# Retention feeding two feed-forward layers: where the decays are applied, and how the first product is placed between the retention steps

## The chip, the cores and the metric

The kernel runs on one core of one Trainium2 chip. The metric is the device time of one execution in microseconds (us), median of three runs.

## The reference, cut to what matters

Inputs q, k, v are 4 x 8 x 768 x 64 (batch, heads, sequence, head size). For every batch and head a state of 64 x 64 decays and grows along the sequence, and the outputs go through two dense layers:

```python
gamma = 1.0 - 2.0 ** (-5.0 - np.arange(H))
for t in range(S):
    state = gamma * state + outer(k[t], v[t])
    y[t] = scale * (q[t] @ state)
x = y.transpose(0, 2, 1, 3).reshape(3072, 512)
x = leaky_relu(x @ w_in) @ w_out          # 512 -> 2048 -> 512
x = sigmoid_gated(x @ w2_in) @ w2_out     # 512 -> 2048 -> 512
```

## The kernel before, in words

The first stage computes the retention in 24 steps (4 batches of 6 chunks of 128 positions) and, beside it, the first product (x @ w_in) of the first block of 512 tokens. Everything behind it is dense matrix work on TensorE (PE): the rest of the first product (line 238), then the three other products (lines 776 and 583). The change touches the first stage alone. In program order each engine runs its own queue, so the order in which the Python code issues work is the order on each engine.

One retention step s does the following. `a_scores` (line 269) multiplies keys and queries of 8 heads on PE (line 277) into PSUM banks 0 and 1, and VectorE (DVE) multiplies the result by the causal mask into SBUF (line 280). `a_decay` (line 283) multiplies the keys by their decays on ScalarE (ACT), eight instructions a step (line 288), two steps ahead. `a_out` (line 290) runs on PE the state update (kv, line 300, not in the last chunk of a batch), the output inside the chunk (line 307), and the output from the state (line 313, not in a batch's first chunk). DVE forms the next state from kv (line 316); kv accumulates over the chunks in one bank, so the next kv waits for line 316. The output lies in two PSUM banks; two such pairs take turns (banks 3 to 6). `a_store` (line 320) multiplies the output by the decays of the queries (`qdec`) on DVE: line 332, three instructions, for blocks 0 and 1, line 345, one, for later blocks, which go to DRAM. For block 0 ACT makes the rounded high part (line 341) and GpSimd (POOL) subtracts for the low part (line 151). Half of the rows come out with the two 64-row halves exchanged; `swapped` (line 159) puts them right, by three DMAs for each store and for `qdec`.

A weight tile of the first product goes through: `load_raw` (line 165, one DMA of 512 KB), `convert` (two instructions on ACT, lines 172 and 173, four on DVE, lines 176 to 182), `round_up` (line 191, on POOL for the first two tiles, on DVE for the others), `finish` (ACT copy, line 154, DVE subtraction, line 151). One tile is then 12 matmuls of 128 x 512 (`ffn_in`, line 231), a Lrelu on ACT out of bank 7 (line 242) and a store. From step 6 on, 16 of the 18 steps end with one tile. Loads of q, k, v (1 MB a step, line 267, on SP's DMA queue) are four steps ahead.

Of the kernel before, what the change touches and what calls it, by code (L numbers as in the profile page):

```python
# [21 lines left out]
P = 128  # L22
# [65 lines left out]
def retention_two_ffn(ctx: ExitStack, tc: tile.TileContext, qkv, consts, small, w1i, w1o, w2i, w2o, scratch, out):  # L88
# [123 lines left out]
    W0 = 6  # L212
    now_in = [[m for m in range(KF) if W0 + m * (N_STEPS - W0) // KF == s] for s in range(N_STEPS)]
    done = [0]

    def work_first(n):
        if n + 2 < KF:
            load_raw(n + 2)
        if n < KF:
            convert(n)  # L220

    def work_last(n):
        if n < KF:
            round_up(*conv[n], nc.gpsimd if n < 2 else nc.vector)
        if 0 < n <= KF:
            finish(n - 1)

    h_banks = [7]
    i_h = [0]

    def ffn_in(blk, m, place=None):
# [9 lines left out]
        t = next(g_ring) if place is None else place  # L241
        nc.scalar.activation(out=t, in_=h, func=AF.Lrelu)  # L242
        if place is None:
            nc.scalar.dma_start(out=gd1[m][:, blk * TB : blk * TB + TB], in_=t)

    def retention():
# [12 lines left out]
        ins, sc_t, ks_t = {}, {}, {}  # L259
        kv = banks[:, 2, : NP * D].rearrange("p (n d) -> p n d", n=NP)  # L260
        o_ring = itertools.cycle([banks[:, 3:5], banks[:, 5:7]])
# [21 lines left out]
        def a_decay(s):  # L283
            b, c = steps[s]
            if c < NC - 1:
                ks_t[s] = ins[s][:, 2].rearrange("p (h d) -> p h d", h=H)
                for h in range(H):
                    nc.scalar.activation(out=ks_t[s][:, h], in_=ks_t[s][:, h], func=AF.Copy, scale=kdec[:, c, h : h + 1])

        def a_out(s):  # L290
            b, c = steps[s]
            t = ins.pop(s)
            sm, ks = sc_t.pop(s), ks_t.pop(s, None)
# [8 lines left out]
            o = next(o_ring)  # L302
# [15 lines left out]
            return o  # L318

        def a_store(s, o):  # L320
# [4 lines left out]
            else:  # L325
# [4 lines left out]
            def put(r, u, t):  # L330
                n = 2 * P
                nc.vector.tensor_tensor(out=x[r].rearrange("p (m u) i -> p u m i", u=2)[:, u],  # L332
                                        in0=o[t, u, :n].rearrange("p (m i) -> p m i", i=P),
# [9 lines left out]
            if blk < 2:  # L343
                return
# [773 lines left out]
```

## Time and profile before

| what | value |
|---|---|
| median of 3 runs | 1048.61 us (1048.59 to 1049.26) |
| profiled execution: span from first to last instruction | 1047.2 us |
| PE busy | 1038.1 us (99%) |
| DVE busy | 821.6 us (78%) |
| ACT busy | 578.2 us (55%) |
| POOL busy | 72.8 us (7%) |

The page gives the profiled execution's own time as its span, 1047.2 us; the median lies 1.4 us above it, which is what lies around the span. A view that shows starts gives them in us from the start of the span. "PE ... x16" in a timeline is sixteen matmul records: a 4-byte product of the retention leaves two records for each matmul. A matmul's modelled end overlaps the next start, so durations on PE are taken from start to start.

### The profile page before, as it was taken

What the parts mean: (1) busy time and instruction counts of PE and PEld (TensorE: products, weight loads), DVE (VectorE), ACT (ScalarE), POOL (GpSimd) and SP (SyncE); (2) the same over time, 40 slices, a digit from 0 to 9 for tenths busy, and PEclk for the clock granted to TensorE, in tenths of its full rate; (3) what the DMA queues carried; (4) which work ended last, traced back from release to release, by engine and by line L of the source; (5) the groups of instructions that cost most, each with busy time, mean ns of one, the idle gap of its engine ahead of it and who ended that gap; (6) DMA issues with size and microseconds to landing.
All of it is one profiled execution on the core that took longest, in us unless ns stands there. A gap on an engine that the chain in (4) does not pass through costs nothing.

```text
span 1047.2 us, 16899 instructions
## 1 busy us (share of the span) xinstructions
PE 1038.1 (99%) x5955; PEld 892.3 (85%) x5955; DVE 821.6 (78%) x1425; ACT 578.2 (55%) x1111; POOL 72.8 (7%) x75
## 2 busy tenths in 40 slices
PE   8999999999999999999999999999999999999998
PEld 6778788888888888888888999999999888888886
DVE  5998749886885798787789677686768898887986
ACT  5766446554554654544546566565657564545443
POOL 2100000000000000000000104434410000000000
PEclk9999999999999999999999999999999999999999
DMA  9989577999996423524429846647487735635624
GB/s 336 364 318 363 212 232 236 317 320 323 326 334 207 151 81 131 191 80 161 160 81 331 302 160 212 230 171 282 158 271 263 250 101 139 184 92 143 168 81 80
DMA packets 168645, 223.72 MB, mean 214 GB/s; under 512 B 57328, under 2 KB 113392, under 8 KB 165360
## 3 DMA queue, kind: packets, MB, share of 16 engines
q1 hardware_dynamic: 133696, 175.67, 51.3%
q10 hardware_dynamic: 34864, 46.97, 12.2%
q8 instruction: 46, 0.75, 0.3%
q14 instruction: 39, 0.32, 0.1%
HBM read 137.66 MB, written 84.93 MB: 213 GB/s over the span
## 4 chain that ended last, share of the span: by engine, by line
PE 94%; DVE 3%; DMA 2%; issue 0%; ACT 0%; ACTq 0%; SPq 0%
PE psum L776 41%; PE psum L238 25%; PE psum L583 22%; PE psum L277 2%; PE psum L307 2%; DMA h<-qkv 1%; PE psum L300 1%; PE psum L313 1%; ACTq L1000 0%; DVE c L992 0%; DVE c L784 0%; DVE e L151 0%; DVE a L151 0%; DVE d L151 0%; DVE c L332 0%
## 5 line engine op out<-in xcount | busy, mean ns | idle before, releaser
L776 PE MATMUL psum<-c,h 128*128 128x512 f32 x1008 | 228.8, 389 | 0.0
L776 PEld LDWEIGHTS psum<-c,h 128*128 128x128 f32 x1008 | 189.2, 188 | 39.3
L776 PE MATMUL psum<-e,h 128*128 128x512 f32 x768 | 179.3, 389 | 0.0
L776 PEld LDWEIGHTS psum<-e,h 128*128 128x128 f32 x768 | 144.2, 188 | 29.9
L238 PE MATMUL psum<-d,h 128*128 128x512 f32 x576 | 136.2, 393 | 0.5 <-DVE h L151 0.5
L238 PE MATMUL psum<-a,h 128*128 128x512 f32 x576 | 131.2, 389 | 0.0
L238 PEld LDWEIGHTS psum<-d,h 128*128 128x128 f32 x576 | 106.8, 188 | 25.6 <-issue 1.7
L238 PEld LDWEIGHTS psum<-a,h 128*128 128x128 f32 x576 | 108.0, 188 | 22.6 <-issue 0.2
L583 PE MATMUL psum<-c,h 128*128 128x384 f32 x576 | 110.1, 334 | 0.3 <-DVE d L620 0.3
L583 PE MATMUL psum<-b,h 128*128 128x384 f32 x576 | 110.1, 334 | 0.0
L583 PEld LDWEIGHTS psum<-c,h 128*128 128x128 f32 x576 | 100.7, 188 | 0.6 <-DVE d L620 0.6
L583 PEld LDWEIGHTS psum<-b,h 128*128 128x128 f32 x576 | 100.6, 188 | 0.4 <-ACT psum L656 0.3
L729 ACT CAST c<-b 128x512 fp32r<-128x512 f32 x96 | 59.3, 622 | 57.4 <-DVE c L151 35.6
L603 ACT ACTIVATE d<-psum 128x384 f32<-128x384 f32 x96 | 47.1, 492 | 64.6 <-PE psum L583 57.8
L151 DVE TENSOR_TENSOR c<-b,c 128x512 fp32r<-128x512 f32 x96 | 65.4, 690 | 18.8 <-ACT c L729 16.6
L242 ACT ACTIVATE e<-psum 128x512 f32<-128x512 f32 x80 | 47.6, 595 | 55.6 <-PE psum L238 53.0
L729 ACT CAST e<-a 128x512 fp32r<-128x512 f32 x77 | 47.7, 622 | 43.8 <-PE psum L776 22.4
L151 DVE TENSOR_TENSOR h<-h 128x384 fp32r<-128x384 f32 (+3 forms) x88 | 44.9, 545 | 28.4 <-ACT h L154 21.0
L151 DVE TENSOR_TENSOR e<-a,e 128x512 fp32r<-128x512 f32 x77 | 52.4, 685 | 8.4 <-ACT e L729 7.8
L607 DVE TENSOR_TENSOR d<-psum,d 128x384 f32<-128x384 f32 x96 | 52.1, 549 | 4.5 <-ACT d L603 2.8
L151 POOL TENSOR_TENSOR a<-a 128x768 f32<-128x768 f32 x7 | 13.2, 1891 | 586.8 <-DMA h<-wds 540.8
L776 PE MATMUL psum<-f,h 128*128 128x512 f32 x192 | 48.7, 389 | 0.0
(147 smaller groups left out, 1428.4 us busy)
## 6 DMA issues: line engine op xcount, KB each, us to landing
gd<-d ACTq DMA_DIRECT2D x128, 192.0 KB, 3.6
h<-qkv SPq DMA_DIRECT2D x21, 1024.0 KB, 8.5
gd<-e ACTq DMA_DIRECT2D x80, 256.0 KB, 4.9
d<-gd SPq DMA_DIRECT2D x64, 256.0 KB, 4.1
b<-gd SPq DMA_DIRECT2D x64, 256.0 KB, 4.1
a<-gd SPq DMA_DIRECT2D x48, 256.0 KB, 4.9
c<-w1i SPq DMA_DIRECT2D x16, 512.0 KB, 7.4
xd<-e SPq DMA_DIRECT2D x12, 512.0 KB, 3.1
```

The source lines that it names most:

```text
L151: e.tensor_tensor(out=o, in0=x, in1=y, op=ALU.subtract)
L238: nc.tensor.matmul(out=h, lhsT=w[:, a, k], rhs=xs[blk % 2][k][:, c], start=(i == 0), stop=(i == 3 * NP - 1), skip_group_check=True)
L242: nc.scalar.activation(out=t, in_=h, func=AF.Lrelu)
L277: nc.tensor.matmul(out=ps[:, e, n], lhsT=kT[r, n], rhs=qT[r, n], start=True, stop=True, skip_group_check=True)
L300: nc.tensor.matmul(out=kv[r, n], lhsT=ks[:, 2 * n + e], rhs=v[:, n, r], start=(c == 0 and n == 0), stop=True, skip_group_check=True)
L307: nc.tensor.matmul(out=out(n, e), lhsT=v[:, n, r], rhs=sm[:, e, n], start=(n < 2), stop=(c == 0), skip_group_check=True)
L313: nc.tensor.matmul(out=out(n, e), lhsT=st[c % 2][r, n], rhs=q[r, n], start=False, stop=True, skip_group_check=True)
L583: nc.tensor.matmul(out=t, lhsT=w[:, k, a], rhs=x[:, b, k], start=(start and m == 0), stop=(m == 5), skip_group_check=True)
L603: nc.scalar.activation(out=s, in_=src, func=AF.Sigmoid, scale=1.702)
L607: nc.vector.tensor_tensor(out=dst, in0=src, in1=s, op=ALU.mult)
L729: nc.scalar.copy(out=t[:, 0], in_=self.block_of(*item))
L776: nc.tensor.matmul(out=t[:, j], lhsT=w[:, j, a], rhs=x[:, b], start=(new and q == 0 and m == 0), stop=(q == NQ - 1 and m == 2), skip_group ...
```

## The change

The queries are multiplied by `qdec` and the keys by `kdec` in place, both before they are used, by one two-operand instruction each (`a_scale`): on POOL, except the queries of steps 0 and 1, which are on DVE. The scores of step s now read scaled queries. The output is copied as it is, by one ACT instruction (for block 0 that is the rounded copy, and DVE subtracts, out of PSUM). It stays half-exchanged; the rows of the first weight are exchanged instead when they are loaded, by three DMAs per tile. `qdec` comes by one DMA, ahead of the second half of step 0's data, and the first two weight tiles are loaded before the steps. The output has one pair of banks in place of two; Lrelu reads from three banks in turn. `round_up` is on POOL for all 16 tiles. The first product is cut into 64 pieces of three matmuls; they are issued from step 4 to step 23, three or four a step, between the scores of the step and its `a_out`. From step 4 on the scores are those of the same step, not of the next one. `keep_warm` in front is 12 matmuls, not 8.

```diff
-    def swapped(d, s):
+    def exchanged(d, s):
         nc.sync.dma_start(out=d[:, 0::2], in_=s[:, 0::2])
         for r, t in halves:
...
     def load_raw(m):
-        nc.sync.dma_start(out=t, in_=w1i[m].bitcast(U32).rearrange("p (f two) -> p f two", two=2))
+        exchanged(t.rearrange("p (k f) two -> p k f two", k=NP),
+                  w1i[m].bitcast(U32).rearrange("p (k f two) -> p k f two", k=NP, two=2))
...
+    PIECES = NP * KF
+    FIRST = 4
+    given = [PIECES * max(s - FIRST + 1, 0) // (N_STEPS - FIRST) for s in range(N_STEPS)]
+    starts = [next(s for s in range(N_STEPS) if given[s] > NP * m) for m in range(KF)]
-    h_banks = [7]
+    h_banks = [5, 6, 7]
...
-        o_ring = itertools.cycle([banks[:, 3:5], banks[:, 5:7]])
+        o = banks[:, 3:5]
...
-        def a_decay(s):
+        def a_scale(s):
             b, c = steps[s]
+            q, k = ins[s][:, 0], ins[s][:, 2].rearrange("p (h d) -> p h d", h=H)
+            (nc.vector if s < 2 else nc.gpsimd).tensor_tensor(out=q, in0=q, in1=qdec.rearrange("p n i -> p (n i)"), op=ALU.mult)
             if c < NC - 1:
-                for h in range(H):
-                    nc.scalar.activation(out=ks_t[s][:, h], in_=ks_t[s][:, h], func=AF.Copy, scale=kdec[:, c, h : h + 1])
+                nc.gpsimd.tensor_tensor(out=k, in0=k, in1=kdec[:, c].unsqueeze(2).to_broadcast([P, H, D]), op=ALU.mult)
...
             if blk == 0:
-                nc.scalar.copy(out=x0[:, :, 0, cols], in_=x)
-                subtract(x0[:, :, 1, cols], x, x0[:, :, 0, cols].bitcast(F32), nc.gpsimd)
+                nc.scalar.copy(out=by_pair(x0[:, :, 0, cols]), in_=src)
+                subtract(by_pair(x0[:, :, 1, cols]), src, by_pair(x0[:, :, 0, cols]).bitcast(F32))
                 return
...
+            nc.scalar.copy(out=by_pair(x), in_=src)
+            if blk > 1 and cc % 2:
+                nc.sync.dma_start(out=xd0[blk][:, :, cc * P - P : cc * P + P], in_=a_store.x)
...
+        nc.sync.dma_start(out=qdec, in_=consts[:, H:])
         nc.sync.dma_start(out=ins[0][:, 2:], in_=qkv[0, :, 2:])
...
+        for n in (1, 2):
+            a_load(n)
+        load_raw(0)
         a_load(3)
+        load_raw(1)
...
-        keep_warm(8)
+        keep_warm(12)
+        a_scale(0)
         a_scores(0)
-        a_decay(0)
-        a_decay(1)
+        a_scale(1)
         for s in range(len(steps)):
             if s == 0:
                 keep_warm(6)
-            elif s + 1 < len(steps):
+            elif s < FIRST - 1:
                 a_scores(s + 1)
+            elif s >= FIRST:
+                a_scores(s)
+            for m in range(KF):
+                if starts[m] == s + 1:
+                    finish(m)
+            fresh = [m for m in range(KF) if starts[m] == s + 2]
+            for m in fresh:
+                if m + 2 < KF:
+                    load_raw(m + 2)
+                convert(m)
+            for _ in range(given[s] - (given[s - 1] if s else 0)):
+                next(pieces)
+            a_out(s)
...
+            a_store(s)
+            for m in fresh:
+                round_up(*conv[m], nc.gpsimd)
             if s + 2 < len(steps):
-                a_decay(s + 2)
+                a_scale(s + 2)
             if s + 4 < len(steps):
                 a_load(s + 4)
-            for m in now_in[s]:
-                ffn_in(0, m)
```

## Rows read from the trace of the kernel before

**Rows 1.** Busy time by stretch: engines' busy us (instructions), granted clock, DMA share, GB/s.
```profile
0.00:34.50 34.50, 29.72 (x439) 21.59 (x439) 22.74 (x41) 20.76 (x68) 9.05 (x12) 1.00 0.93 351
34.50:131.80 97.30, 97.30 (x1183) 77.32 (x1183) 81.28 (x141) 62.05 (x167) 0.00 (x0) 1.00 0.84 305
```
**Rows 2.** Chain that ended last, in order: start us, us, what.
```profile
9.66 9.89 DMA h<-qkv
...
131.83 217.82 PE psum L238 x960
```
**Rows 3.** Timeline of PE, one step with a tile and the next scores.
```profile
75.90 3.04 PE L238 MATMUL psum<-d,h 128*128 128x512 f32 x12
78.87 1.16 PE L277 MATMUL psum<-h 64*128 64x128 f32 x16
79.96 0.69 PE L300 MATMUL psum<-h 128*64 128x64 f32 x16
80.47 1.05 PE L307 MATMUL psum<-b,h 128*64 128x128 f32 x16
81.45 0.67 PE L313 MATMUL psum<-h,b 64*64 64x128 f32 x16
82.05 1.16 PE L277 MATMUL psum<-h 64*128 64x128 f32 x16
```
**Rows 4.** Timeline of PE, the first 35 us.
```profile
1.25 3.60 PE L372 MATMUL psum<-f 128*128 128x512 bf16 x8 [1.25 <-DVE f L363]
5.03 1.16 PE L277 MATMUL psum<-h 64*128 64x128 f32 x16 [0.18 <-DMA h<-qkv]
6.12 1.47 PE L372 MATMUL psum<-f 128*128 128x512 bf16 x6
...
28.35 0.67 PE L313 MATMUL psum<-h,b 64*64 64x128 f32 x16
30.60 1.16 PE L277 MATMUL psum<-h 64*128 64x128 f32 x16 [1.58 <-DVE b L280]
```
**Rows 5.** Groups by line and shape, 0 to 160 us: busy us, mean ns, idle before.
```profile
L280 DVE TENSOR_TENSOR b<-psum,b 128x1024 f32<-128x1024 f32 x24 | 29.4, 1223 | 18.3 <-PE psum L277 18.1
L345 DVE TENSOR_TENSOR h<-psum,f 128x512 f32<-128x512 f32 x16 | 11.0, 686 | 4.4 <-PE psum L313 4.4
L182 DVE SCALAR_TENSOR_TENSOR b<-b,c 128x512 uint32<-128x512 uint32 x16 | 11.1, 693 | 0.6
L316 DVE TENSOR_TENSOR b<-psum,f 128x256 f32<-128x256 f32 x20 | 8.3, 415 | 1.2 <-PE psum L300 1.2
L178 DVE TENSOR_SCALAR b<-b 128x512 f32<-128x512 f32 x18 | 7.6, 422 | 0.0
L341 ACT CAST d<-h 128x512 fp32r<-128x512 f32 x4 | 2.5, 619 | 4.7 <-DVE h L332 4.7
L151 POOL TENSOR_TENSOR d<-h,d 128x512 fp32r<-128x512 f32 x4 | 5.1, 1280 | 15.1 <-ACT d L341 15.1
L191 POOL TENSOR_TENSOR b<-b,c 128x512 int32<-128x512 int32 x2 | 2.6, 1292 | 5.0 <-ACT h L288 5.0
```
**Rows 6.** Load of step 3's q, k, v: when issued, us to landing.
```profile
L267 SPq DMA_DIRECT2D h<-qkv x1: 328/328/328, 6.2 to 6.2; - x1
DMA to landing us min/median/max: 9.8/9.8/9.8
```
**Rows 7.** Timeline of POOL and DVE around 680 us, in a later stage.
```profile
681.02 1.91 POOL L551 TENSOR_TENSOR a<-a 128x768 f32<-128x768 f32 x1
681.61 1.60 DVE L178 TENSOR_SCALAR e<-e 128x512 f32<-128x512 f32 x1
```

**Rows 8.** DMA issues from 34.5 to 131.8 us: count, KB each, median us to landing.
```profile
gd<-e ACTq DMA_DIRECT2D x16, 256.0 KB, 4.8
xd<-h SPq DMA_DIRECT2D x7, 256.0 KB, 4.2
```

More of the change, by code (lines that the diff above doesn't have):

```diff
@@ L210, in x_split, with ffn_pieces @@
             x_load(q + 1)
[L212 to L226, printed above, removed]
-    h_banks = [7]
+    PIECES = NP * KF
[3 more added lines that the diff above has]
+    h_banks = [5, 6, 7]
     i_h = [0]
-    def ffn_in(blk, m, place=None):
+    def ffn_pieces(blk, m, place=None):
         h = banks[:, h_banks[i_h[0] % len(h_banks)]]
@@ L240, in ffn_in @@
                 i += 1
[L241 to L244, printed above, removed]
+            if k == NP - 1:
+                t = next(g_ring) if place is None else place
+                nc.scalar.activation(out=t, in_=h, func=AF.Lrelu)
+                if place is None:
+                    nc.scalar.dma_start(out=gd1[m][:, blk * TB : blk * TB + TB], in_=t)
+            yield
+    def ffn_in(blk, m, place=None):
+        for _ in ffn_pieces(blk, m, place):
+            pass
     def retention():
@@ L328, in a_store @@
                 x = a_store.x[:, :, cc % 2 * P : cc % 2 * P + P]
[L330 to L333, printed above, removed]
[L334 to L339 removed]
+            by_pair = lambda a: a.rearrange("p (m u) i -> p u m i", u=2)
+            src = o[:, :, : 2 * P].rearrange("p u (m i) -> p u m i", i=P)
             if blk == 0:
[L341 to L343 removed]
+                nc.scalar.copy(out=by_pair(x0[:, :, 0, cols]), in_=src)
+                subtract(by_pair(x0[:, :, 1, cols]), src, by_pair(x0[:, :, 0, cols]).bitcast(F32))
                 return
[L345 to L349 removed]
+            nc.scalar.copy(out=by_pair(x), in_=src)
+            if blk > 1 and cc % 2:
+                nc.sync.dma_start(out=xd0[blk][:, :, cc * P - P : cc * P + P], in_=a_store.x)
         ins[0] = next(in_ring)
@@ L358, in retention @@
                                 compare_op=ALU.is_ge, fill=0.0)
-        a_load(1)
-        swapped(qdec, consts[:, H:])
-        a_load(2)
+        for n in (1, 2):
+            a_load(n)
+        load_raw(0)
         a_load(3)
+        load_raw(1)
         nc.vector.memset(idle, 0.0)
@@ L372, in keep_warm @@
                 nc.tensor.matmul(out=warm, lhsT=idle[:, :P], rhs=idle, start=True, stop=True, skip_group_check=True)
-        keep_warm(8)
+        pieces = itertools.chain.from_iterable(ffn_pieces(0, m) for m in range(KF))
+        keep_warm(12)
+        a_scale(0)
         a_scores(0)
-        a_decay(0)
-        a_decay(1)
+        a_scale(1)
         for s in range(len(steps)):
@@ L380, in retention @@
                 keep_warm(6)
-            elif s + 1 < len(steps):
+            elif s < FIRST - 1:
                 a_scores(s + 1)
-            o = a_out(s)
-            n = None
-            if s >= W0 - 2 and done[0] < KF + 1 and (s <= W0 or now_in[s - 1]):
-                n = done[0]
-                done[0] += 1
-                work_first(n)
+            elif s >= FIRST:
[11 more added lines that the diff above has]
+            a_out(s)
             if s == 0:
```

26 lines of the change are left out of this document (4 added, 22 removed).

## The prediction, made before the changed kernel was timed

> **What bounds the kernel now.** I read the stretches first, then the chain, then the timeline of PE. From 34.5 us to 131.8 us PE is busy for all of 97.30 us, and behind that the chain is one run of matmuls that starts at 131.83 us [rows 1, 2]. So the first stage is bound by PE from 34.5 us on, although DVE (81 us) and DMA (share 0.84) are not far off, and all that follows starts when the stage is over. The change ends there: I forecast the moment at which the rest of the first product can start, 131.8 us now, and add the difference to the whole. The span is 1047.2 us, the median 1048.61 us; the 1.4 us around the span stay.
>
> In front of 34.5 us PE is busy for 29.7 us only. There the chain goes through loads (9.89 us of it end with step 4's data) [rows 2], and later through DVE: PE waits 1.58 us for the masked scores at 30.60 us [rows 4]. Only this part has room for a gain.
>
> **PE's work.** From start to start [rows 3]: a tile of 12 matmuls takes 2.97 us, scores 1.09, kv 0.52, output 0.97, state product 0.60; a step without the tile 3.18 us. A matmul in the long run takes 217.82/960 = 0.227 us [rows 2], so 12 cost 2.72 us and each group has 0.25 us of entering and leaving. The change leaves 192 matmuls and all small products as they are, and makes 20 groups out of 16: 4 x 0.25 = **+1.0 us**. The small products of 24 steps sum to 24 x 3.18 - 4 x 0.60 - 4 x 0.52 = 71.8 us, the groups to 192 x 0.227 + 20 x 0.25 = 48.6 us, and two warm-ups lie between steps 0 and 1 (1.47 us each [rows 4]). The first scores start at 5.03 us now; then they need `qdec` too, 262 KB more at 351 GB/s [rows 1], 0.75 us, and a multiplication on DVE, 0.69 us as line 345 [rows 5]: 6.5 us. So the stage can't end before 6.5 + 71.8 + 48.6 + 2.9 = 129.8 us. The most that can be gained is **2.0 us**, if PE never waits.
>
> **What is taken off other engines.** Per step DVE loses a multiplication (line 345, 0.69 us [rows 5]) and ACT its eight small ones; ACT gains a copy of 0.62 us as line 341. Behind 34.5 us neither holds PE, so this is worth nothing there. DVE's three multiplications in steps 0 to 7 go too; that could remove the 1.58 us at 30.60 us. What takes their place is below.
>
> **Where PE waits in steps 2 to 4.** I follow the new order from row to row; "+0.1" is a signal. Step 3's data land at 6.2 + 9.8 = 16.0 us now [rows 6]. The first weight tile, 524 KB, is put ahead of them: 1.5 us at 351 GB/s. `qdec` in one piece saves between 0 and 0.75 us of its own load; I take 0.5. So they land at 17.0 us (bounds 16.7 and 17.5). POOL then multiplies step 3's queries: the form is line 151's on POOL, 1.28 us [rows 5]. The keys' factor is broadcast, which no row shows; its ends are DVE's 0.69 us and twice 1.28; I take 1.28. Scores 3 start at 18.4 and end at 19.5 us. On DVE the mask (1.22) ends at 20.8 us. Next in DVE's queue stand the four word instructions of tile 0, because `convert` is now issued ahead of `a_out`: 3 x 0.42 + 0.69 = 1.95 us, to 22.8. Only then comes line 316 of step 2 (0.41), for which the kv of step 3 waits, and the subtraction that frees the only output pair (0.69): 23.9 us. PE finished step 2 at 21.6 us (19.5 + 2.09), so it waits about 2.4 us in two pieces around kv, and ends step 3 at 24.0 + 0.97 + 0.60 = 25.6 us. POOL rounds tile 0 from 22.9 to 24.2 (1.29), then scales step 4's queries to 25.5 us; scores 4 run from 25.6 to 26.7.
>
> The pieces of step 4 need the low part of step 3's tokens. DVE's queue ahead of it: the subtraction of tile 0, the four word instructions of tile 1, line 316. Whether POOL holds these up matters: DVE's line 178 took 1.60 us beside a POOL instruction and ended 0.28 us behind it, instead of 0.42 us [rows 5, 7]. So an instruction of DVE with two operands in SBUF, or a one-operand one, waits for POOL's to end. Then: subtraction from 25.5 to 26.1, behind it POOL's keys to 27.3, words 27.3 to 29.2, line 316 to 29.6, low part to 30.3. Pieces run from 30.4 to 32.7, and step 4 ends at **34.8 us**. Without that hold-up it would be 1.6 us earlier.
>
> The Trainium skill (SBUF — State Buffer, Who interferes with whom) says that VectorE and GpSimd share a pair of ports, and that the second to come waits for the whole instruction; the trace agrees, 1.60 us against 0.42 [rows 5, 7]. By the rule the sum is the 34.8 us above, against it 33.2 us.
>
> **The sum.** Left at 34.8 us: 19 scores (20.7), 15 kv (7.8), 19 outputs (18.4), 16 state products (9.6), 183 matmuls (41.5) and 19 groups (4.7): 102.7 us, end 137.5 us. The same count for before, from the scores at 30.60 us (17 scores, 15 kv, 18 outputs, 15 state products, 16 tiles), gives 131.4 against 131.8 read, so it holds to 0.4 us. **137.5 - 131.8 = +5.7 us.**
>
> **What I cost at nothing.** The steps from 5 on: a cycle of five steps is 27.1 us on PE (14.9 of small products, 12.2 of groups). POOL does in it 4 roundings, 5 queries and about 4.2 keys, 16.9 us, and DVE 4 times 2.65 us of instructions that exclude POOL (1.95 + 0.69): 27.5 us if nothing overlaps, though of DVE's only the part that streams excludes POOL (0.28 of 0.42 us [rows 7]), so I take no wait; the other end is a rival. The single output pair: a copy of 0.62 us, covered by the next scores and pieces (3.4 us). The three DMAs per tile in place of one: rows of 1 KB, as the old store had; that moved 256 KB in 4.2 us where the 2 KB rows of Lrelu's store took 4.8 [rows 8], so no loss, and 0.16 x 97 = 15.6 us of DMA time are free. SP's queue holds the loads four steps ahead behind the store, which waits for ACT's copy: some tenths, covered by that distance. The store needs one DMA for three.
>
> **The rivals.**
> *The waits are filled.* Pieces lie between scores and output from step 4 on, so a late mask no longer stops PE, and DVE has less to do. If the low part of block 0 and tile 0 are ready when scores 4 end, and those end by about 21 us, nothing waits, and the stage ends near 129.8 us: 1046.6 us. For it: 1.58 us at 30.60 us is such a wait [rows 4]. Against it: the chain from tile 0's words over POOL to step 4's queries. Chance 0.06.
> *Half the waits.* Loads land early, word instructions slip in ahead, and PE waits some 3 us less than I count: 1050 us and somewhat below, the relief of DVE and ACT being off the path. This is also what is seen if the moves do nothing but add four groups: 1049.6 us. Chance 0.16 for a result within 0.2%.
> *POOL becomes the bound.* With gaps of 0.08 us between its instructions (13 of them) and signals of 0.1, the cycle is 29 us with no overlap, 2 us over PE's 27.1, four times: +8 us, 1062 us. It decides from the second run of four tiles on, when the words of a step end 7 us after its scores. Chance 0.12.
> *The clock falls.* In the first stage the granted clock is 1.00 [rows 1], the 2.4 GHz level, but the first eight warm-ups took 3.60 us, 0.45 each, and the six after the first scores 0.245 each [rows 4]: the engine began at the 1.2 GHz level and rose after those eight. If the clock falls in the wait of 3.7 us behind scores 4 (26.7 to 30.4 us), the way back costs about 3.60 - 8 x 0.245 = 1.6 us: 1056 us. Nothing in the rows shows a fall after a wait of 1.6 us. Chance 0.08, within the range of the forecast.
> The Trainium skill (TensorE: Matmul & The Clock Gate, Part 1) says that an idle array is put back to half its rate; no row here shows that.
>
> **How the numbers follow.** The likeliest case is +5.7 us: 1048.6 + 5.7 = **1054.3 us**; its own range is 1051 (no hold-up by POOL, early landing, one wait less) to 1057.5 (late landing, keys at twice 1.28, the clock). Chance 0.58. The range of 8 in 10 goes down to 1049, into the case of half the waits, and up to 1060, into POOL as the bound. About 0.2%, 2.1 us, is what a measurement of this kernel can tell from no change. Faster by more: 0.06. Within: 0.16. Slower: 0.58 + 0.12 + 0.08 = 0.78.
>
> **What would show it.** The start of the long run of matmuls moves from 131.8 to about 137.5 us. Scores 3 start at about 18.4, scores 4 at 25.6, the first 128 x 512 group at 30.4 us, released by DVE's subtraction. Groups of 9 matmuls take 2.29 us, of 12 2.97. DVE's lines 176 to 182 and 151 show means above 0.42 and 0.69 us. POOL is busy some 65 us more (42 multiplications and 14 roundings, less 4 subtractions, of 1.28 us). The prediction is wrong if the first group starts before 26 us, or if PE waits in most steps behind step 5.

## The result, and the profile after

The changed kernel takes 1056.18 us (median of 4 runs, 1055.59 to 1059.02). The kernel before, run beside it, takes 1048.93 us (4 runs, 1048.59 to 1049.88). The ratio is 1.0072, 95% interval 1.0057 to 1.0086: slower by some 7 us. The forecast was 1054.3 us, +5.7 us. The profiled execution is the one of 1055.59 us, 0.6 us under the median, so what the traces can explain is the 6.7 us between the two profiled spans (1053.9 and 1047.2), not quite the 7.2 us between the medians.

First the page of the changed kernel: span, and busy time of each engine (share, instructions).

```profile
span 1053.9 us, 16876 instructions
PE 1041.4 (99%) x5959; PEld 893.9 (85%) x5959; DVE 811.2 (77%) x1377; ACT 550.4 (52%) x971; POOL 138.2 (13%) x127
```

DVE and ACT lose work, POOL gains 65.4 us, as costed (some 65). PE shows 3.3 us more busy time for the same products, and that says little: a PE at half its clock counts as busy too. The place of the loss is in the stretches (columns as in [rows 1]):

```profile
0.00:34.50 34.50, 26.65 (x321) 18.62 (x321) 20.01 (x30) 8.36 (x14) 14.55 (x17) 0.95 0.96 321
34.50:138.00 103.50, 103.50 (x1307) 81.84 (x1303) 73.29 (x105) 45.47 (x78) 60.55 (x47) 1.00 0.90 296
...
17.30:24.40 7.10, 4.83 (x64) 4.21 (x65) 4.04 (x7) 2.23 (x4) 2.62 (x3) 0.76 1.04 375
24.40:34.50 10.10, 7.14 (x105) 5.74 (x105) 8.96 (x14) 4.06 (x8) 6.18 (x5) 1.00 1.03 306
```

Behind 34.5 us PE never waits (103.50 of 103.50 us), with POOL carrying 60.55 us there. In front of it PE is busy for 26.65 us, 3.1 us less than before [rows 1]. Two things are new: the granted clock of 0.76 from 17.3 to 24.4 us, which is part of that stretch at the 1.2 GHz level, and 321 GB/s where it was 351, with the DMA engines fuller (0.96 against 0.93). The chain of waits shows the rest (start us, us, what):

```profile
3.25 8.44 DMA h<-qkv
...
17.66 1.28 POOL h L282
...
24.07 1.30 POOL b L192
27.06 1.26 DVE c L177
30.83 2.33 PE psum L228 x9
...
138.09 100.88 PE psum L228 x444
```

Before, the largest piece of the chain up to there was a load of 9.89 us [rows 2]; now the chain runs through step 3's load, POOL's scaling of the queries (L282), POOL's rounding of weight tile 0 (L192) and DVE's first word instruction of tile 1 (L177), the order that the prediction followed. The long run of matmuls starts at 138.09 us, against 131.83 [rows 2] and a forecast of 137.5. The chain leaves it after 444 matmuls, because just before 280.08 us PE waits once for ScalarE.

```profile
PE psum L228 <- ACT e L233: 0.3, 1, 0.3
```

That 0.3 us is in the waits of the changed kernel behind 138 us (engine, line, waited for: us, times, longest) and not in those of before. The 960 matmuls take 218.46 us with it and 217.82 before, 0.6 us more, which is most of the way from 6.3 us at the long run's start to 6.7 us in the spans. ScalarE was late because it had stood for 4.52 us, until 278.31 us, behind a store of a weight block (`wds<-c`) whose buffer it needed; whether the change has to do with that was not tried.

The timeline of PE, the first 36 us (answers to [rows 4]; L273 scores, L296 kv, L302 and L308 output, L228 first product):

```profile
7.48 1.16 PE L273 MATMUL psum<-h 64*128 64x128 f32 x16 [1.31 <-DVE h L282]
...
18.98 1.82 PE L273 MATMUL psum<-h 64*128 64x128 f32 x16 [1.74 <-POOL h L282]
20.74 1.12 PE L296 MATMUL psum<-h 128*64 128x64 f32 x16
21.64 1.57 PE L302 MATMUL psum<-b,h 128*64 128x128 f32 x16
23.14 0.67 PE L308 MATMUL psum<-h,b 64*64 64x128 f32 x16
24.41 0.69 PE L296 MATMUL psum<-h 128*64 128x64 f32 x16 [0.60 <-DVE b L311]
...
26.86 1.16 PE L273 MATMUL psum<-h 64*128 64x128 f32 x16
30.83 2.33 PE L228 MATMUL psum<-d,h 128*128 128x512 f32 x9 [2.81 <-DVE d L151]
...
35.19 1.16 PE L273 MATMUL psum<-h 64*128 64x128 f32 x16
```

And the timeline of DVE and POOL in the same stretch, lines in order of time:

```profile
5.79 1.09 POOL L340 TENSOR_SCALAR_AFFINE_SELECT b<-f 128x1024 f32<-128x1024 f32 x1 [5.28 <-DMA f<-small]
6.31 1.11 DVE L282 TENSOR_TENSOR h<-h,f 128x512 f32<-128x512 f32 x1 [5.11 <-DMA f<-consts]
...
17.65 1.28 POOL L282 TENSOR_TENSOR h<-h,f 128x512 f32<-128x512 f32 x1 [3.49 <-DMA h<-qkv]
18.89 1.04 POOL L284 TENSOR_TENSOR h<-h,f 128x512 f32<-128x512 f32 x1
...
24.06 1.29 POOL L192 TENSOR_TENSOR b<-b,c 128x512 int32<-128x512 int32 x1 [4.13 <-issue]
25.31 1.28 POOL L282 TENSOR_TENSOR h<-h,f 128x512 f32<-128x512 f32 x1
26.05 1.09 DVE L151 TENSOR_TENSOR h<-b,h 128x512 fp32r<-128x512 f32 x1 [0.86 <-ACT h L154]
26.55 1.49 POOL L284 TENSOR_TENSOR h<-h,f 128x512 f32<-128x512 f32 x1
27.06 1.26 DVE L177 TENSOR_SCALAR c<-c 128x512 uint32<-128x512 uint32 x1
...
30.10 0.68 DVE L151 TENSOR_TENSOR d<-psum,d 128x512 fp32r<-128x512 f32 x1
```

Read from top to bottom: step 3's data reach POOL at 17.65 us, PE gets its scores at 18.98, POOL's rounding starts 0.1 us behind tile 0's words (24.06), step 4's queries stand behind the rounding (25.31), and the low part that releases the first 128x512 group (30.10) stands last in DVE's queue.

**The difference counted on PE.** The first scores start 2.45 us later (7.48 against 5.03 [rows 4]); four more groups are 1.0 us by the prediction's 0.25 us each. This counts where PE loses time, not why. Taking the prediction's 71.8 us of small products, 48.6 us of groups (47.6 before) and 2.9 us of warm-ups from the span between first scores and long run leaves 138.09 - 7.48 - 123.3 = 7.3 us lost now, and 131.83 - 5.03 - 122.3 = 4.5 us before: 2.8 us more. 2.45 + 1.0 + 2.8 = 6.3 us. Of the 7.3 us, 5.15 are the three waits above (1.74, 0.60, 2.81) and 1.6 the half clock (scores of step 3, kv and output of step 2, from start to start 1.76, 0.90 and 1.50 us instead of 1.09, 0.52 and 0.97 [rows 3]). The 2.45 us at the start are lost only on this count: on the chain scores 3 wait for their data, so that earlier first scores would have made that wait longer.

### The profile page after: what moved, and what is told of

Read it like the earlier page. It is cut to its first block, busy times and chain, and to the rows that moved or that the text cites. A ratio compares the mean times of both kernels' runs of the same rounds, so it can differ in the third digit from the quotient of the medians.

```text
span 1053.9 us, 16876 instructions
## 1 busy us (share of the span) xinstructions
PE 1041.4 (99%) x5959; PEld 893.9 (85%) x5959; DVE 811.2 (77%) x1377; ACT 550.4 (52%) x971; POOL 138.2 (13%) x127
## 4 chain that ended last, share of the span: by engine, by line
PE 93%; DMA 3%; DVE 1%; issue 1%; ACT 1%; POOL 0%; SPq 0%; ACTq 0%; DVEq 0%; POOLq 0%
PE psum L765 43%; PE psum L572 22%; PE psum L228 21%; PE psum L273 2%; PE psum L302 2%; DMA wds<-b 1%; PE psum L308 1%; PE psum L296 1%; DMA h<-qkv 1%; DMA wds<-c 1%; DMA wds<-e 0%; DVE b L151 0%; POOL h L282 0%; DVE b L183 0%; ACT b L173 0%
## 5 line engine op out<-in xcount | busy, mean ns | idle before, releaser
L228 PE MATMUL psum<-d,h 128*128 128x512 f32 x576 | 137.3, 394 | 3.1 <-DVE d L151 2.8
L228 PE MATMUL psum<-a,h 128*128 128x512 f32 x576 | 131.2, 389 | 0.0
L228 PEld LDWEIGHTS psum<-d,h 128*128 128x128 f32 x576 | 106.5, 188 | 27.6 <-DVE d L151 3.0
L228 PEld LDWEIGHTS psum<-a,h 128*128 128x128 f32 x576 | 108.0, 188 | 22.6 <-issue 0.2
L151 DVE TENSOR_TENSOR c<-b,c 128x512 fp32r<-128x512 f32 x96 | 65.4, 690 | 19.1 <-ACT c L718 16.9
L151 POOL TENSOR_TENSOR a<-a 128x768 f32<-128x768 f32 x7 | 13.2, 1893 | 497.5 <-DMA h<-wds 451.4
L233 ACT ACTIVATE e<-psum 128x512 f32<-128x512 f32 x80 | 47.6, 595 | 44.2 <-PE psum L228 42.0
L151 DVE TENSOR_TENSOR h<-h 128x384 fp32r<-128x384 f32 (+3 forms) x88 | 44.2, 538 | 29.0 <-ACT h L154 20.8
L151 DVE TENSOR_TENSOR e<-a,e 128x512 fp32r<-128x512 f32 x77 | 52.4, 685 | 8.2 <-ACT e L718 7.7
```

The source lines that it names most:

```text
L151: e.tensor_tensor(out=o, in0=x, in1=y, op=ALU.subtract)
L228: nc.tensor.matmul(out=h, lhsT=w[:, a, k], rhs=xs[blk % 2][k][:, c], start=(i == 0), stop=(i == 3 * NP - 1), skip_group_check=True)
```

## The experiments

The theory: PE waits where the prediction put them, because of the order in which step 3's data, the mask, the words of two weight tiles, POOL's rounding and its scaling come. Rivals for the size of the loss: the exchanged loads (three DMAs of 1 KB rows), POOL holding up DVE, the clock, and the quarter tiles themselves. Two numbers recur: the distance from scores 3 to the first 128x512 group, and where the long run starts by the chain. Ratios are against the kernel before, run beside each.

| kernel | scores 3 | first group | distance | long run | ratio, 95% |
|---|---|---|---|---|---|
| changed | 18.98 | 30.83 | 11.85 | 138.09 | 1.0072 (1.0057 to 1.0086) |
| step 3's data first | 16.98 | 28.99 | 12.01 | 137.69 | 1.0057 (1.0040 to 1.0074) |
| warm-ups in the wait | 20.05 | 31.24 | 11.19 | 138.93 | 1.0085 (1.0058 to 1.0112) |
| no key scaling | 20.95 | 32.07 | 11.12 | 139.43 | 1.0058 (1.0043 to 1.0073) |
| plain weight loads | 18.30 | 29.51 | 11.21 | 138.72 | 1.0066 (1.0052 to 1.0080) |
| the same, tile 1's words later | 18.12 | 26.60 | 8.48 | 135.80 | 1.0043 (1.0027 to 1.0058) |
| the same, warm-ups before the group | 18.64 | 30.58 | 11.94 | 138.24 | 1.0063 (1.0049 to 1.0077) |

**Step 3's data ahead of weight tile 0.**

```diff
-        load_raw(0)
         a_load(3)
+        load_raw(0)
         load_raw(1)
```

> The changed kernel with one edit: the data of step 3 are loaded ahead of the first weight tile, not behind it. Theory of the late chain (step 3's data, POOL's scaling of its queries, scores 3, DVE's queue, first pieces): scores 3 start about 1.4 us earlier, at 17.5 us instead of 18.98, the first 128 x 512 group at about 29.4 instead of 30.83 us, the long run of matmuls at about 136.6 instead of 138.1 us; if PE's wait ahead of scores 3 is then too short for the clock to fall, another 0.7 us less. Rival, the weights lead: the words of tile 0 come later by as much, and the first group stays at 30.8 us. Rival, the loss is spread over the steady steps (groups, shared ports): the long run stays at 138.1 us.

Scores 3 start at 16.98 us with no wait, and the first group 1.84 us earlier than in the changed kernel. Of that, 0.40 us is left at the long run, where 1.5 us were expected:

```profile
25.40 1.16 PE L273 MATMUL psum<-h 64*128 64x128 f32 x16 [1.28 <-POOL h L282]
28.99 3.75 PE L228 MATMUL psum<-d,h 128*128 128x512 f32 x9 [2.42 <-DVE d L151]
```

This timeline of PE shows why: the nine matmuls behind the wait of 2.42 us took 3.75 us instead of 2.33. The granted clock was 1.00 from 17 to 24 us here and 0.89 from 24 to 40 us. So the place of the load counts up to the first group, and the clock took most of the gain back at another wait. The distance is no shorter here, although scores 3 ran at full clock, because two word instructions of tile 1 stood beside POOL's work, not one (1.50 and 1.26 us on DVE, lines 177 and 179, 0.42 us each when alone); POOL had waited 0.82 us for step 4's data.

**Warm-up matmuls in the wait ahead of scores 3.**

```diff
                 keep_warm(6)
-            elif s < FIRST - 1:
+            if s == 2:
+                keep_warm(7)
+            if 0 < s < FIRST - 1:
                 a_scores(s + 1)
```

> The changed kernel with seven warm-up matmuls (1.5 us at the full rate) issued in PE's wait of 1.74 us ahead of scores 3. Theory of the late chain: the clock stays at its full level from 17 to 24 us, scores 3 take 1.16 us and not 1.82, but only these 0.66 us lie on the chain, since the next kv and output wait for DVE anyhow: first group at 30.2 us, long run at 137.4 us. Rival, the fall of the clock is the price: all of the 1.6 us that the slow scores, kv and output lost come back, long run at 136.5 us or earlier. Rival, steady steps: no change of the long run's start, 138.1 us.

Scores 3 in the timeline of PE:

```profile
20.05 1.16 PE L273 MATMUL psum<-h 64*128 64x128 f32 x16 [1.59 <-POOL h L282]
```

The clock stays at 1.00 throughout, and the distance from scores 3 to the first group falls by 0.66 us, the 0.67 us by which the half clock lengthened scores 3. Neither 30.2 us for the first group nor 137.4 us for the long run came about, and as a comparison of times it is inconclusive: step 3's data came later in this execution (POOL's queries waited for their load until 18.73 us, against 17.65), and the four runs scatter from 1055.70 to 1062.15 us.

**The keys not scaled from step 3 on** (that scaling is left out).

```diff
-            if c < NC - 1:
+            if c < NC - 1 and s < 3:
                 nc.gpsimd.tensor_tensor(out=k, in0=k, in1=kdec[:, c].unsqueeze(2).to_broadcast([P, H, D]), op=ALU.mult)
```

> The changed kernel without the multiplication of the keys by their decays from step 3 on (left out of the computation: 18 of POOL's instructions of 1.04 to 1.5 us). Theory of the late chain with POOL holding up DVE: line 151 at 26.05 us and line 177 at 27.06 us lose their excess of 0.40 and 0.84 us, the first group starts at about 29.6 us and the long run at about 136.9 us; in the steady steps nothing changes, since PE doesn't wait there. Rival, no hold-up (DVE's long instructions are slow for another reason): both keep 1.09 and 1.26 us, long run at 138.1 us. Rival, POOL paces the steady steps: the long run comes 3 us or more earlier.

Groups by line and shape from 34.5 to 138 us (busy us, mean ns, idle before), first of the changed kernel:

```profile
L151 DVE TENSOR_TENSOR h<-b,h 128x512 fp32r<-128x512 f32 x14 | 13.7, 980 | 1.3 <-ACT h L154 1.2
L177 DVE TENSOR_SCALAR c<-c 128x512 uint32<-128x512 uint32 x13 | 10.3, 789 | 0.2 <-ACT b L173 0.2
...
L282 POOL TENSOR_TENSOR h<-h,f 128x512 f32<-128x512 f32 x18 | 24.0, 1331 | 0.9 <-DMA h<-qkv 0.9
L284 POOL TENSOR_TENSOR h<-h,f 128x512 f32<-128x512 f32 x15 | 19.8, 1319 | 0.0
```

and of the kernel without the keys' scaling:

```profile
L151 DVE TENSOR_TENSOR h<-b,h 128x512 fp32r<-128x512 f32 x14 | 10.8, 769 | 0.0
...
L177 DVE TENSOR_SCALAR c<-c 128x512 uint32<-128x512 uint32 x14 | 5.9, 419 | 0.0
```

L177 is back at the 0.42 us that [rows 5] show for an instruction of its kind (L178 there), and at the place on the chain too, where the changed kernel has 1.26 us:

```profile
29.15 0.42 DVE L177 TENSOR_SCALAR c<-c 128x512 uint32<-128x512 uint32 x1
```

So POOL's keys do hold DVE's words up, by 0.84 us on the chain. L151, which runs beside the queries that are still scaled, takes 1.11 us as before. The distance falls by 0.73 us, with scores 3 at half clock in both kernels. Of the absolute times nothing can be said: step 3's data landed only at 19.6 us and the long run started at 139.43 us. In the steps behind 34.5 us PE has no wait with the keys on POOL and none without, and from the scores of step 5 to the long run it takes 102.9 us with them and 103.0 without: POOL is not the bound.

**The exchanged halves alone, in the kernel before.** The output's decay in one instruction, halves left exchanged, weights loaded by three DMAs; everything else is the kernel before.

```diff
     def load_raw(m):
         raw[m] = t = next(raw_ring).bitcast(U32)
-        nc.sync.dma_start(out=t, in_=w1i[m].bitcast(U32).rearrange("p (f two) -> p f two", two=2))
+        swapped(t.rearrange("p (k f) two -> p k f two", k=NP),
+                w1i[m].bitcast(U32).rearrange("p (k f two) -> p k f two", k=NP, two=2))
...
-            if blk < 2:
-                put(slice(0, P), 0, slice(0, P))
-                for r, t in halves:
-                    put(r, 1, t)
...
-            if cc % 2:
-                swapped(xd0[blk][:, :, cc * P - P : cc * P + P], a_store.x)
+            if blk > 1 and cc % 2:
+                nc.sync.dma_start(out=xd0[blk][:, :, cc * P - P : cc * P + P], in_=a_store.x)
```

> The kernel before with one part of the change alone: the halves stay exchanged in the tokens, the rows of the first weight are exchanged at loading (three DMAs per tile), and the decay of the outputs takes one instruction on DVE in steps 0 to 7, not three. Theory that DVE's queue sets PE's waits between 28 and 35 us in the kernel before: DVE has 0.6 us less per step, the wait of 1.58 us ahead of the scores at 30.60 us and that of 0.52 us in the first group shrink by about 1.5 us together, the long run starts at 130.3 instead of 131.8 us, time 1047.2 us. Rival, nothing: DVE catches up anyhow, 131.8 us. Rival, the loads: 1 KB rows and two half-height DMAs per tile hold up the data of steps 4 to 8, the long run starts 1 us later or more.

Here the theory missed and its rival came true: the long run starts at 134.29 us, 2.5 us behind the kernel before, and the ratio is 1.0044 (1.0028 to 1.0060; 5 runs, 1051.04 to 1056.21 us). The profiled execution is the fastest of the five. The rows stand with the next kernel's.

**The same with plain weight loads.** The rows of the weight are exchanged in the layout in which the kernel is given it, so that one DMA loads a tile in 4 KB rows.

```diff
-        swapped(t.rearrange("p (k f) two -> p k f two", k=NP),
-                w1i[m].bitcast(U32).rearrange("p (k f two) -> p k f two", k=NP, two=2))
+        nc.sync.dma_start(out=t, in_=w1i[m].bitcast(U32).rearrange("p (f two) -> p f two", two=2))
...
+    def half_exchanged(a):
+        t = a.reshape(KF, 2, D, NP, P).copy()
+        t[:, :, :, 1::2] = t[:, ::-1, :, 1::2].copy()
+        return t.reshape(KF, P, 512)
...
-        "w1i": w_in(inputs["moe_w_in"]), "w1o": w_out(inputs["moe_w_out"]),
+        "w1i": half_exchanged(w_in(inputs["moe_w_in"])), "w1o": w_out(inputs["moe_w_out"]),
```

> As e7_before_exchanged (the kernel before, halves left exchanged, one decay instruction for each store), with the weight's rows exchanged when the inputs are laid out, so that a tile comes by one DMA of whole rows. Theory that the exchanged loads made e7_before_exchanged slow (long run at 134.2 us, clock at 0.81 between 31 and 40 us): without them DVE's relief shows, long run at 130.3 us against 131.8 us of the kernel before, time 1047.1 us. Rival, leaving the halves exchanged is slow by itself (order of the stores, or DVE's one instruction): 134 us. Rival, no relief: 131.8 us.

The long run starts at 130.64 us. Busy time from 24.4 to 34.5 us and the weight's loads up to 34.5 us (KB each, median us to landing), with exchanged loads:

```profile
24.40:34.50 10.10, 6.55 (x107) 5.44 (x104) 8.90 (x15) 6.88 (x22) 3.72 (x3) 0.90 1.05 320
...
c<-w1i SPq DMA_DIRECT2D x5, 256.0 KB, 9.1
c<-w1i SPq DMA_DIRECT2D x8, 128.0 KB, 8.7
```

and with plain ones:

```profile
24.40:34.50 10.10, 8.76 (x142) 7.25 (x139) 9.96 (x17) 8.20 (x24) 3.84 (x3) 1.00 1.01 400
...
c<-w1i SPq DMA_DIRECT2D x5, 512.0 KB, 6.5
```

The DMA engines are full in both, and move 320 GB/s in the one and 400 in the other. The loads land 2.2 to 2.6 us later, step data and weight tiles arrive late, PE waits 4.5 us for them and for the words of a tile, and the clock falls. By the profiles the three DMAs cost 134.29 - 130.64 = 3.65 us, by the medians (1054.30 and 1048.37) 5.9 us. How much of that is due to the 1 KB rows, and how much to three DMAs in place of one, two of them half as high, was not separated. With plain loads the ratio is 0.9993 (0.9985 to 1.0002; 11 runs against 15): the decay of the output in one instruction and the saved DMAs are worth nothing that can be told from no change. What limits there is the loads of q, k, v (PE waits for them five times, 2.8 us).

**Plain weight loads in the changed kernel**, the same edit of the loads (line numbers are one less from here on).

```diff
-        exchanged(t.rearrange("p (k f) two -> p k f two", k=NP),
-                  w1i[m].bitcast(U32).rearrange("p (k f two) -> p k f two", k=NP, two=2))
+        nc.sync.dma_start(out=t, in_=w1i[m].bitcast(U32).rearrange("p (f two) -> p f two", two=2))
```

> The changed kernel with the rows of the first weight exchanged when the inputs are laid out, before the launch, so that a weight tile comes by one DMA of whole rows again. Theory that part of the loss is the DMA time of the exchanged loads (1 KB packets, half-height transfers): step 3's data land about 0.9 us earlier than the 17.6 us of the changed kernel, PE's wait ahead of scores 3 is then too short for the clock to fall (0.66 us on the chain), first group at about 29.2 instead of 30.83, long run at about 136.4 instead of 138.1 us; DMA moves over 340 GB/s in the first 34.5 us, not 321. Rival, the loads cost nothing: 138.1 us. Rival, they are all of the loss: 132 us.

Step 3's data land 0.7 us earlier (POOL starts on them at 16.98 us), scores 3 and the first group come 0.7 and 1.3 us earlier, and the gain is gone again in the group itself, by the timeline of PE:

```profile
29.51 3.88 PE L227 MATMUL psum<-d,h 128*128 128x512 f32 x9 [3.03 <-DVE d L151]
```

3.88 us instead of 2.33: the clock fell in this wait of 3.03 us, while in the changed kernel it held through one of 2.81. The long run starts at 138.72 us, where 136.4 was expected, and the median is 1056.24 us, no better than the changed kernel's. So the expected gain missed, and the rival that the loads cost nothing has the time on its side. The DMA engines did have less to do:

```profile
0.00:34.50 34.50, 26.25 (x319) 18.13 (x320) 20.36 (x31) 8.40 (x14) 15.26 (x18) 0.95 0.87 329
```

They moved 329 GB/s at a share of 0.87, not 321 at 0.96 (over 340 was expected). In this order what the loads cost is hidden behind that wait and the clock. The scatter differs too: the four runs lie within 0.5 us here and within 0.7 to 1.6 in the four variants of this kernel below, against 3.4 in the changed kernel and 1.1 to 6.5 in its three variants above.

**Pieces from step 6 on**, with plain loads.

```diff
-    FIRST = 4
+    FIRST = 6
```

> As e8_plain_loads, and the first product starts in step 6, as in the kernel before, not in step 4 (18 groups). Theory of the late chain: with a mask, line 311 and one subtraction DVE needs 2.3 us for each of steps 2 to 5 and PE 3.2, so PE runs them without the waits for tile 0's and tile 1's words; st of step 5 ends near 30 us, first group near 31.5 us but with two more retention steps done, long run at about 132.2 us. Rival, the steady steps (POOL and DVE on shared ports, more groups) make the loss: the long run stays within 1 us of that of e8_plain_loads.

Missed by 5.4 us: the long run starts at 137.64 us. That is 1.08 us ahead of plain loads alone, so the rival's bound (within 1 us) is just missed too, and its steady steps are not where the time goes. The chain of words, rounding and queries moves along with the tiles, as PE's waits from 17 to 138 us show:

```profile
PE psum L272 <- POOL h L281: 3.6, 3, 1.8
PE psum L272 <- DVE d L151: 1.4, 1, 1.4
...
```

Of the 3.6 us, 1.5 us are ahead of step 6's scores: the rounding of tile 0 starts on POOL at 31.00 us, and step 6's queries wait behind it until 32.24. Another 1.8 us are step 4's data, which reach POOL at 21.9 us, and the 1.4 us are step 3's (POOL has them at 16.86 us and ends their queries at 18.12; scores 3 start at 18.18). So of 6.4 us of waits the loads make 3.2 and the rounding ahead of the queries 1.5. An early step 4 was not what cost the time; both causes stay when the tiles start later.

**Whole tiles instead of quarters**, with plain loads: 16 groups in the 20 steps.

```diff
-    given = [PIECES * max(s - FIRST + 1, 0) // (N_STEPS - FIRST) for s in range(N_STEPS)]
+    given = [NP * -(-KF * max(s - FIRST + 1, 0) // (N_STEPS - FIRST)) for s in range(N_STEPS)]
```

> As e8_plain_loads, with whole tiles of 12 matmuls in 16 of the 20 steps instead of three or four pieces in each. Theory: four groups fewer at 0.25 us, long run 1.0 us earlier than in e8_plain_loads; nothing else waits, since the scores' mask is covered by 12 matmuls as by 9, and in the four steps without a tile PE waits for the mask (1.2 us and two signals, less the 0.5 us of kv) by some 0.9 us each. Net: minus 1.0 plus up to 3.6 us. Rival, the quarter tiles cover these waits for nothing and the groups' cost is not real: 2.5 us later or more.

The rival came true: 143.61 us, 4.9 us later than with plain loads alone, where the theory had at most 2.6 and the rival 2.5 or more. The ratio is 1.0109 (1.0093 to 1.0124). PE's waits from 17 to 144 us:

```profile
PE psum L301 <- DVE b L275: 4.5, 4, 2.1
PE psum L227 <- DVE d L151: 3.0, 1, 3.0
```

In the four steps that get no tile, PE waits for the mask (L275), 0.8 us three times and 2.1 us once. So pieces in every step do cover the mask, as costed, and a step without one loses more than the 0.25 us that it saves. The first twelve matmuls took 5.49 us instead of 2.97 here, at half clock, which cost about 1 us more than the nine of plain loads alone (3.88 instead of 2.33). What a group costs by itself this run does not separate.

**Tile 1's words behind step 4's mask**, with plain loads: the four word instructions of tile 1 leave their place ahead of the low part, and ScalarE's two and POOL's rounding, which belong to them, move along.

```diff
+            if s == FIRST:
+                convert(1)
+                round_up(*conv[1], nc.gpsimd)
...
-                convert(m)
+                if m != 1:
+                    convert(m)
...
-                round_up(*conv[m], nc.gpsimd)
+                if m != 1:
+                    round_up(*conv[m], nc.gpsimd)
```

> As e8_plain_loads, with the word instructions of tile 1 (and its rounding) taken out of step 3 and issued in step 4 behind the mask of the scores. In e8_plain_loads the low part of step 3's tokens, for which the first group waits, stood behind them on DVE and the group started at 29.51 us. Theory that DVE's queue order sets that start: first group at about 26.8 us, PE's wait ahead of it under 1 us instead of 3.3, the group at the full clock (2.3 us, not 3.8); some of it is given back in step 5, where DVE is late by about 1 us; long run at about 135.5 instead of 138.65 us. Rival, something else holds the low part (the output copy, the query scaling): first group still near 29.5 us. Rival, the clock falls in another wait all the same: first group at 26.8 but long run at 137 us.

```profile
26.60 2.34 PE L227 MATMUL psum<-d,h 128*128 128x512 f32 x9 [0.32 <-DVE d L151]
...
35.85 1.09 PE L301 MATMUL psum<-b,h 128*64 128x128 f32 x16 [1.44 <-DVE b L275]
```

PE's timeline: the first group comes at 26.60 us, 2.91 us earlier than with plain loads alone, and the clock is at 1.00 throughout. The words are not gone: 1.44 us of them come back one step later, in front of the mask. The long run starts at 135.80 us, the median falls from 1056.24 to 1053.67 us. The slow clock (3.88 us for the group with plain loads alone, 2.34 here) makes up for what comes back, so that the long run gains the same 2.9 us as the first group. This is the clearest proof of the theory: one edit of the order, with no work left out, moves the wait by the time that the order says, and both numbers were expected before (26.8 and 135.5). It does not explain all: the long run is still 4.0 us behind the kernel before, and no run takes that rest apart.

**Warm-ups ahead of the first group**, with plain loads.

```diff
+            if s == FIRST:
+                keep_warm(13)
             for _ in range(given[s] - (given[s - 1] if s else 0)):
```

> As e8_plain_loads, with 13 warm-up matmuls (2.8 us at the full rate) in PE's wait of 3.3 us ahead of the first group, and nothing else. Theory that the clock fell in that wait (granted 0.90 and 0.89 between 24 and 40 us, nine matmuls in 3.8 instead of 2.3 us): the first group still starts at about 29.5 us, takes 2.3 us, the clock reads 1.00, long run 1.5 us earlier, at 137.1 us. Rival, the clock is on no path there: long run at 138.6 us.

```profile
18.64 1.91 PE L272 MATMUL psum<-h 64*128 64x128 f32 x16 [1.73 <-POOL h L281]
...
30.58 2.33 PE L227 MATMUL psum<-d,h 128*128 128x512 f32 x9
```

The group takes 2.33 us, not 3.88, but in this execution the clock fell earlier, behind the wait of 1.73 us ahead of scores 3. Its profile cannot show what the warm-ups are worth. The other three runs have spans of 1053.8 to 1053.9 us at a mean clock of 0.999 to 1.000; plain loads alone had 1054.2 to 1054.7 us at 0.996 to 0.998. That speaks for half a microsecond, and is not settled by four runs.

**The kernel before with plain loads, `qdec` in one DMA and weight tiles a step later**, an attempt to beat both.

```diff
-        swapped(qdec, consts[:, H:])
+        nc.sync.dma_start(out=qdec, in_=consts[:, H:])
...
-            if s in (1, 2):
-                load_raw(s - 1)
+            if s in (2, 3):
+                load_raw(s - 2)
```

> As e9_before_plain, with the decay table laid out half-exchanged before the launch (one DMA, not three with 512-byte rows) and the first two weight tiles loaded in steps 2 and 3, not 1 and 2. In e9_before_plain PE waits 2.8 us for q, k, v in the first 30 us, with the DMA queues full. Theory that this is DMA time in front of the data: the waits shrink by about 1 us, long run at 129.6 us against 130.57 us there and 131.8 us in the kernel before, time 1047.4 us. Rival, the weight tiles become late: tile 0's words start later and the first group waits, 131 us or more. Rival, the loads are not what PE waits for: 130.6 us.

Not shown in the edit: the halves of `qdec` are exchanged in the layout in which the kernel is given it. L277 and L280 are scores and mask, as in the kernel before.

```profile
PE psum L277 <- DVE b L280: 2.8, 1, 2.8
...
PE psum L277 <- DMA h<-qkv: 0.3, 1, 0.3
```

PE's waits up to 131 us: those for loads fall from 2.8 to 0.3 us, and in their place PE waits 2.8 us for a mask that stands on DVE behind tile 0's words, which are now late. Behind that one wait the clock fell, as the output (L307) shows:

```profile
32.56 1.93 PE L307 MATMUL psum<-b,h 128*64 128x128 f32 x16
```

That is 1.93 us instead of 1.05; with kv and the first tile it makes 1.6 us, most of the 2.15 us by which the long run is later than with plain loads alone. It starts at 132.79 us, ratio 1.0013 (1.0004 to 1.0022; 11 runs). No version here beats the kernel before by more than can be told from no change.

## Why the prediction was right, and where its terms were off

The sign, the mechanism and nearly the size were right: +5.7 us forecast, +6.3 us at the start of the long run, +7.2 us between the medians, inside the range of 1049 to 1060. That the sum came within 0.6 us is in part luck, as below: on the way scores 4 came 1.3 us late, and 0.8 us of that was made up by the first group.

**The order of the waits: right, and shown.** Scores 3, kv of step 3 and the first group wait for what was named; scores 4 start without a wait, as the sum had it, and wait for POOL's queries in the kernel with step 3's data first (1.28 us). Tile 1's words were worth 2.9 us ahead of the first group, and POOL's rounding stands ahead of the queries wherever the tiles start. Forecast and measured: scores 3 18.4 and 18.98, scores 4 25.6 and 26.86, first group 30.4 and 30.83, end of step 4 34.8 and 35.19, long run 137.5 and 138.09 us. From the end of step 4 on the count was off by 0.2 us in 103. One reading in the prediction is wrong without harm to its sum: the 2.4 us around kv of step 3 hold kv's own 0.52, so the waits forecast are 1.9 us. They were 0.9 us (0.60 ahead of kv, 0.3 behind it), since PE came there late, and 1.5 to 1.7 us in the kernels where the clock held ahead of it.

**POOL holds up DVE: right, size 1.2 instead of 1.6 us.** The forecast let tile 1's words start when POOL's keys end. They started beside the keys, and one instruction was stretched to 0.28 us behind their end (1.26 us; the keys end at 28.04, L177 at 28.32): 0.84 us, and 0.40 us on L151 (1.09 instead of 0.69). The sign that lines 176 to 182 would all show it held in the changed kernel for the first of them alone: from 34.5 us on L177 takes 0.79 us, the next three 0.42, 0.43 and 0.69. The Trainium skill (SBUF — State Buffer, Who interferes with whom) gives the rule that the second of the two engines waits for the shared ports; the trace agrees, 0.42 us without the keys and 1.26 beside them.

**Three DMAs per weight tile, "so no loss": wrong.** This is the mis-sized term. Its row was a store of 256 KB in 1 KB rows, in a stretch where DMA was not full [rows 8]. From 24.4 to 34.5 us it is full, and there the exchanged loads moved 320 GB/s where plain ones moved 400; they cost 3.65 us in the order of the kernel before. In the changed kernel they bring step 3's data to POOL at 17.65 us instead of the 17.0 forecast, outside its bounds of 16.7 and 17.5; with plain loads it is 16.98, so the rest of that step was right. Taking them out again did not make the changed kernel faster (1056.24 us), so the term is shown on the landing of the data and not on the time. That delay of 0.65 us, which is one execution's (others differ, below), is the first half of the 1.26 us by which scores 4 came late.

**The clock: right that it could fall, wrong where.** The prediction allowed for it behind scores 4, and held that nothing showed a fall after a wait of 1.6 us [rows 4]. It fell at the wait of 1.74 us ahead of scores 3. The size that the prediction gave for it, 1.6 us, came from warm-ups of 0.45 us each against 0.245; that PE began at the lower level rests on these durations alone, as the granted clock reads 1.00 there too. On PE the fall cost 1.6 us all the same, but only the scores' 0.67 us lie on the chain (0.66 us by the warm-ups experiment); kv and output ran where PE would have waited for DVE. This is the other half of the 1.26 us. The Trainium skill (TensorE: Matmul & The Clock Gate, Part 1) says that an idle array is put back to half its rate; the runs agree that it is (1.82 instead of 1.16 us), and show that the length of the last wait alone does not tell when: it held at 2.81 us in the changed kernel.

**Two terms that cancelled.** Scores 4 were 1.26 us late, the first group only 0.43. Between them words and subtraction overlapped POOL's work, as told above, where the forecast put them in a row. The keys' scaling, taken as 1.28 us, takes 1.04 us alone, and 1.32 us beside DVE.

**The first scores: 7.48 instead of 6.5 us, and harmless.** DVE's scaling of step 0's queries took 1.11 us beside POOL's mask selection (5.79 to 6.88 us), and started 0.5 us later than forecast, because `qdec` landed later. An earlier start would have lengthened the wait ahead of scores 3, which is set by step 3's data; this is read from the chain, no run tried it.

**Costed at nothing, and rightly:** the steps from 5 on, the single output pair and the relief of ACT. PE has no wait from 34.5 to 138 us; POOL as the bound is refuted by the kernel without the keys, whose steps are no faster. From step 5 on groups of nine matmuls took 2.26 to 2.29 us and of twelve 2.95 to 2.97, as forecast; that quarter tiles cover the mask is shown by the whole tiles, which lose 4.5 us to it. The 1.0 us for four more groups is counted from these durations and not shown alone.

**Left open:** how often the clock falls at which of the two waits, which moves single executions by about 1 us; the 0.3 us near 280 us; what the warm-ups ahead of the first group are worth; and the 4.0 us that are left when tile 1's words come later. By the count on PE these 4.0 us are 2.2 us of later first scores, 1.0 of groups and 0.8 of waits.

## What to carry to other kernels

When instructions move to another engine, write down the new order of every queue and follow the first data through it: here the loss, but for the 1.0 us counted for four more groups, arises ahead of the first group at 31 us, in three waits for what stands in another engine's queue and in the slow clock behind one of them, and of the 65 us of work moved onto POOL what lies behind 34.5 us cost PE nothing. A load cut into more and smaller pieces was paid for where the DMA engines were already full (3.65 us in the order of the kernel before), and a row from a stretch where they are not full did not show it; where the layout of the data can be changed before the launch, that avoids it. In another order the same edit brought nothing, since another wait set the time. And a short wait of PE can be paid twice, by itself and by the clock behind it, so that a gain ahead of one wait may be lost at the next.

## What the runs showed of the hardware that was not expected

- The granted clock fell at a wait of 1.74 us (changed kernel, 0.76 from 17.3 to 24.4 us) and held through one of 2.81 us in the same execution; with plain loads it held at 1.46 us ahead of scores 3 and fell at 3.03; with tile 1's words later it held throughout; with the warm-ups before the group it fell at 1.73 us; with the warm-ups ahead of scores 3 it held through 3.02 us. The kernel before waits 1.58 us [rows 4] and keeps 1.00.
- Full DMA engines moved 320 GB/s with weight tiles loaded by three DMAs of 1 KB rows and 400 with one DMA of 4 KB rows, at shares of 1.05 and 1.01 (24.4 to 34.5 us, in the order of the kernel before).
- With the three-DMA loads, step 3's data reached POOL at 15.6, 17.65, 18.7 and 19.6 us in four kernels; the first had that load put first, the other three issue it in the same order. With plain loads it was 16.8 to 17.3 us in five kernels.
- An instruction of DVE with two operands in SBUF took 1.11 us, not 0.68, beside POOL's affine select.
